# One instruction order for a whole gated attention and token-MLP kernel, with half-array projections, a GELU table and transposes by DMA

## The chip, the core and the metric

The kernel runs on one core of one Trainium2 chip, and the metric is the device time of one execution in microseconds. The core has TensorE (PE, the matrix array, which writes to eight banks of PSUM), VectorE (DVE), ScalarE (ACT) and GpSimd (POOL) for the rest of the arithmetic, and SyncE (SP), which here issues most DMA transfers. Each engine runs its own list of instructions in order and waits on semaphores for the others, so an instruction that waits holds back everything behind it on its engine.

## The reference

The input x has 2048 rows (tokens) of 448 features. A gate g mixes two branches, attention with a compressive memory (16 heads of 28 features, four segments of 512 tokens) and an MLP over the token axis after a layer norm:

```python
q, k, v = x @ wq, x @ wk, x @ wv          # split in 16 heads, 4 segments s
phi = lambda t: jnp.where(t > 0, t + 1.0, jnp.exp(t))
...
p = _softmax(qs @ ks.T * scale + causal_mask)
a_dot = p @ vs
a_mem = (phi(qs) @ M) / (phi(qs) @ z + 1e-06)
o = sigmoid(beta) * a_mem + (1.0 - sigmoid(beta)) * a_dot
M = M + phi(ks).T @ vs ; z = z + phi(ks).sum(rows)
...
a = o @ wo
u = _gelu(_layernorm(x).T @ w1 + b1)       # 448 x 1792, contracted over 2048 tokens
b = (u @ w2 + b2).T
g = _sigmoid((x * gate_w).sum(-1))
return g * a + (1 - g) * b
```

(This is the reference shortened; inputs and output are bf16.)

## The kernel before

The program calls `op(engine, function, reads, writes)` for every instruction group in program order; the small scheduler `Sched` derives the semaphores, and each engine's list is simply the order of those calls. So the order of the Python loops is the order on every engine.

There are two parts. **The front** (lines 508 to 536) runs over four blocks `tc` of 512 tokens. For each block `transposes` turns x with products against an identity (L359) and DVE copies the result out (L365); `do_k` and `do_q` (both through `proj_d`, L374) make K and Q with four chained products of 112 rows, transposed, a 512-token block by 128 columns, that is four heads padded from 28 to 32; `do_v` and `do_kt` (both through `proj_t`, L385) make V and a second, untransposed K. phi is computed as an exponential on ACT (L406, L427), a clamp on POOL (L408, L429) and a combine on DVE (L410, L431). `do_mst` (L444) adds phi(k)ᵀv to the memory. PSUM banks are taken in turn from all eight. After the last block `ln_coef` and sixteen `ln_apply` (L498 to L506) normalise x in place on POOL.

**The back half** is a loop of 50 slots. Each slot issues `scores` (L568), four products on four groups of array rows for four heads; then one `exp` over all four banks 0 to 3 on ACT (L577) and one or two causal masks on POOL (L582, L587). Every third slot `pv_unit` adds the product with V (L608, 16 products of 32 columns) and the division on DVE (L616 to L645), which writes the attention output over `qT`. Between them `mlp` issues an even share of 448 products: `mm1` (L656, u = w1ᵀx over 16 token tiles) and `mm2` (L689, y over 14 tiles of u). GELU is built by hand from ACT passes (Square L664, Identity L667, Tanh L675) and DVE passes (L670, L678). `wo_tile` (L720) and `final` (L728) join the branches, and SP stores 16 tiles (L731). The weights W1 and W2 come as 15 blocks of about 1 MB through a ring of five buffers (`ring_load`, L300 and L305).

In the profile most operands are called `t`, so groups are told apart by line.

## Time and profile before

| what | value |
|---|---|
| time, median of 3 runs (lowest to highest) | 258.96 us (258.67 to 259.0) |
| span of the profiled execution | 256.4 us |
| PE busy in the span | 201.7 us (79%) |
| DVE, ACT, POOL busy | 147.3 us, 140.5 us, 83.3 us |
| moved by DMA | 20.19 MB |

The span runs from the first to the last instruction of one profiled execution; the median of the runs is 2.6 us above it. Busy time of PE is not work at full speed: its clock has two levels, 1.2 and 2.4 GHz, which the profile shows as 0.50 and 1.00, and the records of products overlap, so the price of a group is read from the start of one group to the start of the next. Products of DVE, ACT and POOL show their own duration.

### The profile page before, as it was taken

How to read it: one execution, taken by the hardware profiler on the slowest of the kernel's cores; microseconds unless marked ns; L12 is line 12 of the kernel's file. 1: busy time of each engine (PE TensorE's matmuls, PEld its weight loads, DVE VectorE, ACT ScalarE, POOL GpSimd, SP SyncE). 2: the span in 40 equal slices, each digit the busy share in tenths (PEclk: the TensorE clock that was granted, in tenths of full speed). 3: DMA queues.
4: the chain of work that ended last, by engine and by line, in shares of the span. 5: the costliest groups of instructions: out<-in, count | busy, mean ns of one | idle time of the engine just before them, and what ended most of it. 6: DMA issues, size and time to landing. Idle time of an engine off the chain costs nothing.

```text
span 256.4 us, 3519 instructions
## 1 busy us (share of the span) xinstructions
PE 201.7 (79%) x1377; PEld 90.4 (35%) x1389; DVE 147.3 (57%) x265; ACT 140.5 (55%) x180; POOL 83.3 (32%) x122
## 2 busy tenths in 40 slices
PE   0499994996795028998989984995889898899893
PEld 0245551362352001233334431432343343334451
DVE  0426855944854700235567785974986677568703
ACT  0234614532641602389999986776766757756121
POOL 8001112301402099714443542340443223233000
PEclk9999998699799555589999998899999999999999
DMA  6999900000000000032632523145061460100102
GB/s 202 311 257 291 289 10 0 5 0 0 0 3 0 0 1 0 0 102 64 164 94 51 143 62 85 36 111 143 0 182 38 141 179 21 36 20 0 36 3 72
DMA packets 35908, 20.19 MB, mean 79 GB/s; under 512 B 1332, under 2 KB 35892, under 8 KB 35892
## 3 DMA queue, kind: packets, MB, share of 16 engines
q1 hardware_dynamic: 33328, 18.35, 26.5%
q10 hardware_dynamic: 2564, 1.62, 2.6%
q8 instruction: 11, 0.18, 0.3%
q14 instruction: 5, 0.04, 0.1%
HBM read 18.13 MB, written 1.84 MB: 78 GB/s over the span
## 4 chain that ended last, share of the span: by engine, by line
PE 39%; DVE 25%; ACT 18%; POOL 9%; issue 4%; DMA 3%; DVEq 0%; ACTq 0%
PE t L689 13%; ACT t L577 9%; PE t L374 6%; PE t L385 5%; PE t L656 5%; POOL t L506 4%; PE t L720 4%; DVE t L410 3%; DMA t<-in_A_wq_dram 3%; POOL t L408 3%; DVE t L402 3%; ACT t L406 3%; PE t L608 3%; PE t L568 2%; DVE t L728 2%
## 5 line engine op out<-in xcount | busy, mean ns | idle before, releaser
L577 ACT ACTIVATE t<-t 128x2048 bf16<-128x2048 f32 (+1 forms) x48 | 76.5, 1594 | 30.9 <-PE t L568 30.8
L656 PE MATMUL t<-t 128*128 128x448 bf16 x224 | 55.0, 382 | 10.4 <-POOL t L506 8.6
L689 PE MATMUL t<-t 128*128 128x448 bf16 x224 | 46.4, 353 | 0.0
L587 POOL TENSOR_SCALAR_AFFINE_SELECT t<-t 128x512 bf16<-128x512 bf16 x32 | 23.9, 748 | 50.4 <-ACT t L577 50.4
L582 POOL TENSOR_SCALAR_AFFINE_SELECT t<-t 128x512 bf16<-128x512 bf16 x32 | 24.2, 756 | 33.0 <-ACT t L577 31.9
L656 PEld LDWEIGHTS t<-t 128*128 128x128 bf16 x224 | 20.5, 101 | 38.0 <-issue 15.4
L374 PE MATMUL t<-t 112*128 112x512 bf16 x128 | 31.3, 401 | 3.3 <-DVE t L365 3.3
L385 PE MATMUL t<-t 112*128 112x449 bf16 (+1 forms) x112 | 26.7, 393 | 7.9 <-ACT t L406 6.5
L568 PE MATMUL t<-t 28*128 28x512 bf16 (+3 forms) x256 | 18.2, 319 | 16.1 <-ACT t L577 11.2
L689 PEld LDWEIGHTS t<-t 128*128 128x128 bf16 x224 | 20.2, 98 | 20.1 <-issue 2.6
L670 DVE SCALAR_TENSOR_TENSOR t<-t 128x448 f32<-128x448 f32 x14 | 9.2, 661 | 31.2 <-ACT t L667 31.1
L406 ACT ACTIVATE t<-t 128x512 bf16<-128x512 f32 x12 | 7.2, 597 | 27.6 <-DVE t L402 27.6
L728 DVE SCALAR_TENSOR_TENSOR t<-t 128x448 bf16<-128x448 f32 x16 | 10.5, 671 | 17.0 <-PE t L720 14.8
L408 POOL TENSOR_SCALAR t<-t 128x512 bf16<-128x512 bf16 x12 | 7.4, 613 | 38.6 <-ACT t L406 38.6
L374 PEld LDWEIGHTS t<-t 112*128 112x128 bf16 x128 | 12.9, 103 | 19.6 <-issue 3.6
L696 ACT ACTIVATE t<-t 128x448 bf16<-128x448 f32 x16 | 11.6, 722 | 14.7 <-PE t L689 14.7
L385 PEld LDWEIGHTS t<-t 112*128 112x128 bf16 x112 | 11.2, 105 | 21.4 <-DVE t L402 8.1
L410 DVE SCALAR_TENSOR_TENSOR t<-t 128x512 bf16<-128x512 bf16 x12 | 8.3, 692 | 17.9 <-POOL t L408 17.9
L568 PEld LDWEIGHTS t<-t 28*128 28x128 bf16 x256 | 5.2, 92 | 35.4 <-ACT t L577 21.8
L608 PE MATMUL t<-t 128*32 128x512 bf16 (+3 forms) x256 | 12.2, 312 | 6.8 <-DVE t L728 4.8
L429 POOL TENSOR_SCALAR t<-t 128x448 bf16<-128x448 bf16 x12 | 7.4, 616 | 25.9 <-ACT t L427 25.8
L402 DVE CAST t<-t 128x512 bf16<-128x512 f32 x16 | 11.0, 685 | 7.1 <-PE t L374 7.1
(70 smaller groups left out, 236.9 us busy)
## 6 DMA issues: line engine op xcount, KB each, us to landing
t<-in_B_w_dram SPq DMA_DIRECT2D x7, 1024.0 KB, 12.5
t<-in_B_w_dram SPq DMA_DIRECT2D x8, 896.0 KB, 5.1
t<-in_A_x_dram SPq DMA_DIRECT2D x4, 448.0 KB, 8.1
out_dram<-t SPq DMA_DIRECT2D x16, 112.0 KB, 1.7
t<-in_A_wk_dram ACTq DMA_DIRECT2D x1, 392.0 KB, 5.3
t<-in_A_wq_dram ACTq DMA_DIRECT2D x1, 392.0 KB, 7.9
...
```

What stands on the lines that cost most here:

```text
L374: last = e.matmul(bank(b)[:, 0:512], w_pad[0:CK, c, hg * 128 : hg * 128 + 128], xT[0:CK, c, tc * 512 : tc * 512 + 512], start=(c == 0), st ...
L385: last = e.matmul(bank(b)[:, 0:ncol], xT[0:CK, c, t * 128 : t * 128 + 128], w[0:CK, c, 0:ncol], start=(c == 0), stop=(c == NCT - 1), skip_ ...
L402: op("DVE", lambda e: e.tensor_copy(qs, bank(b)[:, 0:512]), reads=[R_bank[b]], writes=[R_qT[hg][tc]], name=f"cpq{tc}_{hg}")
L410: op("DVE", lambda e: e.scalar_tensor_tensor(phq[:, hg, (tc - 1) * 512 : tc * 512], qs, 0.0, eqt[:, p, :], op0=ALU.max, op1=ALU.add), read ...
L568: last = e.matmul(bank(hl)[:, c0 : c0 + w_], kT[r, hg, s * 512 + j * 128 : s * 512 + j * 128 + 128], qT[r, hg, s * 512 + 128 * j : s * 512 ...
L577: op("ACT", lambda e: e.activation(pv, ps[:, 0:4, 0:w], ACT.Exp, scale=SCALE), reads=R_bank[0:4], writes=[R_P[u % 2][f]] + alias, name=f"e ...
L582: op("POOL", lambda e, d=d: e.affine_select(d, d, pattern=[[0, 4], [1, 128]], compare_op=ALU.is_ge, fill=0.0, base=0, channel_multiplier=- ...
L587: op("POOL", lambda e: e.affine_select(d, d, pattern=[[0, 4], [1, 128]], compare_op=ALU.is_ge, fill=0.0, base=0, channel_multiplier=-1), r ...
L608: last = e.matmul(bank(CTX)[32 * hl : 32 * hl + 32, 128 * j : 512], vaug[:, 4 * s + j, 32 * h : 32 * h + 32], pv[:, hl, c0 : c0 + w_], sta ...
L656: op("PE", lambda e: e.matmul(bank(b)[:, 0:D], w1c[:, st, f2 * 128 : f2 * 128 + 128], xh[:, st, :], start=(st == 0), stop=(st == NT - 1), ...
L689: op("PE", lambda e: e.matmul(bank(b)[:, 0:D], w2c[:, ft, t2_ * 128 : t2_ * 128 + 128], uT[:, ft, :], start=(ft == 0), stop=(ft == NFT - 1 ...
L728: op("DVE", lambda e: e.scalar_tensor_tensor(outst[:, p, :], bank(b)[:, 0:D], gcol[:, T : T + 1], ybw[:, T % 4, :], op0=ALU.mult, op1=ALU. ...
```

## The change

The loops are gone. A text `PLAN` lists every step of the kernel once, as `name.arguments@engine`, and a loop at the end calls the function of each step in that order, so the plan alone sets the order on every engine, which engine takes a copy (ACT or DVE) and which PSUM bank or buffer a step uses. The steps themselves change as follows.

- K and Q are made together (`pair`): x is held transposed in both halves of the partitions, 7 chunks of 64 features each, in two different orders (`LC` and `UC`). The product of K runs on array rows 0 to 63 and that of Q on rows 64 to 127, alternating, into two banks. `v` does the same with two token tiles of V. The second projection of K is gone.
- phi is min(max(t,0)+1, exp(t)), on two head groups at a time (1024 columns): `pkm`/`pqm` on DVE or POOL, `pke`/`pqe` on ACT, `pkn`/`pqn` on DVE. phi(k) is turned by a DMA transpose in SBUF (`pkt`, 12 of them).
- x of block 0 is transposed on PE as before (`trx`, 28 products); blocks 1 to 3 are read from HBM with DMA transposes (`xtd`) and copied to the other half of the partitions by plain DMAs (`xtc`).
- Scores are packed into 40 fills of 4 x 512 columns (before 32 of 512 and 16 of 256), each with one `exp` and one mask.
- GELU is one table function over seven tiles of u at once (`gelu`, two calls); u leaves PSUM with its bias on DVE or ACT (`eu`).
- `ea` scales the attention part first and `fin` adds the MLP part; the last y tile is split in two halves of 224 columns.
- Eight products on zeros (`warm`) open the PE list; layer norm is done in four groups, its application shared between POOL and DVE; the ring has three buffers instead of five; PSUM banks 0 to 3 belong to the scores and 4 to 7 to all else.

```diff
+NWARM = 8
...
+LC = (5, 0, 2, 4, 6, 1, 3)
+UC = (6, 1, 3, 5, 0, 2, 4)
+GELU_BATCHES = ((0, 7), (7, 14))
...
+PLAN = """
+warm@P ldwk.0@A dve0@D id@G ldx.0@S ldx.1@S ldwq.0@A setup@G ldwk.1@S acttab@A ldwq.1@S ldsm@S xw.0@D bn.0@D trx.0.3@P
+trx.0.0@P trx.0.2@P trx.0.6@P bn.3@D trx.1.0@P trx.1.6@P trx.1.1@P trx.1.3@P ldwv.0@S trx.1.5@P ex.3@A trx.0.1@P
+xw.1@D trx.0.4@P pad.0@D trx.0.5@P ldwv.1@S trx.1.4@P trx.1.2@P ex.0@D ex.2@A xtd.1@S ex.1@D btr@P0 tb@A pad.1@D
...
+    def xtd(eng, u, tc):
+        b = tc % NXT
+        rows = slice(512 * tc, 512 * tc + 512)
+        dma(eng, xTb[:, b, 1:4, :], x2[rows, 0:384], writes=[R_xT[b][0], R_xT[b][2], R_xT[b][3]], group=f"xt{tc}",
+            transpose=True)
+        dma(eng, xTb[:, b, 0:1, :], x2[rows, 320:448], writes=[R_xT[b][0], R_xT[b][2], R_xT[b][3]], group=f"xt{tc}",
+            transpose=True)
...
+    def xtc(eng, u, tc):
+        b = tc % NXT
+        dma(eng, xTb[half[0], b, 4:7, :], xTb[half[1], b, 0:3, :], reads=[R_xT[b][0]], writes=[R_xT[b][1]],
+            group=f"xc{tc}")
+        dma(eng, xTb[half[1], b, 4:7, :], xTb[half[0], b, 1:4, :], reads=[R_xT[b][0]], writes=[R_xT[b][1]],
+            group=f"xc{tc}")
...
+    def warm(eng, u):
...
+            for _ in range(NWARM):
+                last = e.matmul(bank(7)[:, 0:512], dummy[:, 0:128], dummy[:, 128:640], start=True, stop=True,
                                 skip_group_check=True)
...
-    def proj_d(w_pad, R_w, hg, tc, b):
...
+            for t in (2 * h, 2 * h + 1):
...
-    def do_q(tc, hg):
-        b = next_bank()
-        p = hg % 2
-        proj_d(wq_pad, R_wqp, hg, tc, b)
-        qs = qT[:, hg, tc * 512 : tc * 512 + 512]
-        op("DVE", lambda e: e.tensor_copy(qs, bank(b)[:, 0:512]), reads=[R_bank[b]], writes=[R_qT[hg][tc]],
-           name=f"cpq{tc}_{hg}")
...
+    def pair(eng, u, tc, hg):
+        bk, bq = 4 + u[0], 4 + u[1]
+        slot["k", tc, hg], slot["q", tc, hg] = bk, bq
+        b = tc % NXT
+
+        def fn(e):
+            last = None
+            for i in range(7):
+                for h, c, bb in ((0, LC[i], bk), (1, UC[i], bq)):
+                    last = e.matmul(bank(bb)[:, 0:512], wkq[half[h], c, 128 * hg : 128 * hg + 128], xTb[half[h], b, i, :], start=(i == 0),
+                                    stop=(i == 6), skip_group_check=True)
+            return last
...
+    def v(eng, u, p):
+        t0 = 2 * p
+        bs = (4 + u[0], 4 + u[1])
+        slot["v", t0], slot["v", t0 + 1] = bs
+        b = (t0 // 4) % NXT
+
+        def fn(e):
+            last = None
+            for i in range(7):
+                for h in range(2):
+                    k0 = 128 * ((t0 + h) % 4)
+                    last = e.matmul(bank(bs[h])[:, 0 : D + 1], xTb[half[h], b, i, k0 : k0 + 128],
+                                    wvx[half[h], (LC, UC)[h][i], 0 : D + 1], start=(i == 0), stop=(i == 6),
...
-        op("ACT", lambda e: e.activation(eqt[:, p, :], bank(b)[:, 0:512], ACT.Exp), reads=[R_bank[b]],
-           writes=[R_eqt[p]], name=f"eq{tc}_{hg}")
-        op("POOL", lambda e: e.tensor_scalar(eqt[:, p, :], eqt[:, p, :], 1.0, 0.0, op0=ALU.min, op1=ALU.max),
...
+    def pmax(eng, dst, Rd, T, RT, hp, s):
+        op(eng, lambda e: e.tensor_scalar(dst.rearrange("p (g t) -> p g t", g=2), two(T, hp, s), 0.0, 1.0,
+                                          op0=ALU.max, op1=ALU.add),
+           reads=[RT[2 * hp][s], RT[2 * hp + 1][s]], writes=[Rd])
...
+    def pexp(i, T, RT, hp, s):
...
+    def pmin(dst, Rd, i):
+        op("DVE", lambda e: e.tensor_tensor(dst, dst, et[:, i, :], op=ALU.min), reads=[Rd, R_et[i]], writes=[Rd])
...
+    def pkt(eng, u, s, hg):
+        if hg == 0:
+            slot["kt", s] = u[0]
+        k, i = slot["kt", s], slot["kb", s, hg // 2]
+        dma(eng, phkT[:, k, :, hg * 128 : hg * 128 + 128], phk[:, i, 512 * (hg % 2) : 512 * (hg % 2) + 512],
+            reads=[R_phk[i]], writes=[R_phkT[k][hg]], transpose=True)
...
+    def fill(P, f):
+        a, b = 2 * (P % 2), 2 * (P % 2) + 1
+        return (((a, 0, 0, 512),), ((a, 3, 0, 128), (a, 1, 128, 384)), ((a, 2, 0, 256), (b, 2, 256, 256)),
...
+    def exp(eng, u, P, f):
+        i = slot["P", P, f] = u[0]
+        op("ACT", lambda e: e.activation(punit(i).rearrange("p (a q) -> p a q", a=4), ps[:, 0:4, :], ACT.Exp,
+                                         scale=SCALE),
+           reads=R_bank[0:4], writes=[R_P[i]] + (R_xT[i - NPX] if i >= NPX else []))
```

PE, the start of the program; L359 and `trx` (L518) are transposes, L374 and `pair` (L546) projections of K and Q, L385 and `v` (L571) those of V, L568 and `sc` (L695) scores. Before:

```order
L359 MATMUL t<-t 112x128 x16
L374 MATMUL t<-t 128x512 x32
L359 MATMUL t<-t 112x128 x16
L385 MATMUL t<-t 128x449 x4
L385 MATMUL t<-t 128x448 x4
```

After:

```order
L450 MATMUL t<-t 128x512 x8
L518 MATMUL t<-t 128x128 x28
L463 MATMUL t<-t 128x37
L546 MATMUL t<-t 128x512 x28
L571 MATMUL t<-t 128x449 x14
L546 MATMUL t<-t 128x512 x14
L695 MATMUL t<-t 128x512 x4
L571 MATMUL t<-t 128x449 x14
L546 MATMUL t<-t 128x512 x14
L695 MATMUL t<-t 128x128 x4
L695 MATMUL t<-t 128x384 x4
L546 MATMUL t<-t 128x512 x56
```

In the changed list scores stand between the projections of the first two blocks (from the seventh row on), and the 56 products of block 1 follow the second fill; before, scores begin only behind all four blocks.

SP's DMA queue, from the start (before) and behind the loads of the weights of V (after); `in_B_w_dram` are W1 and W2. Before:

```order
L271 DMA t<-in_A_x_dram 128x4x448 x4
L300 DMA t<-in_B_w_dram 128x16x256 x7
L305 DMA t<-in_B_w_dram 128x14x256 x5
L731 DMA out_dram<-t 128x448
L305 DMA t<-in_B_w_dram 128x14x256
```

After:

```order
L357 DMA_TRANSPOSE t<-in_A_x_dram 128x3x512
L357 DMA_TRANSPOSE t<-in_A_x_dram 128x1x512
L357 DMA t<-in_A_x_dram 128x4x448
L357 DMA t<-t 64x1536 x2
L357 DMA t<-in_B_w_dram 128x16x256
L357 DMA t<-in_A_x_dram 128x4x448
L357 DMA_TRANSPOSE t<-in_A_x_dram 128x3x512
L357 DMA_TRANSPOSE t<-in_A_x_dram 128x1x512
L357 DMA t<-in_A_x_dram 128x4x448
L357 DMA_TRANSPOSE t<-t 128x4x128
L357 DMA t<-t 64x1536 x2
L357 DMA t<-in_B_w_dram 128x16x256
```

The ring's first block (the fifth row) now stands behind a transposed read of x and the two copies that wait for it, and the second block behind a transposed phi(k).

ACT, in the middle of the MLP; L577 and L705 are the exponentials, L664, L667 and L675 the GELU passes, L848 `gelu`, L839 `eu`. Before:

```order
L577 ACTIVATE t<-t 128x1024
L664 ACTIVATE t<-t 128x448
L667 ACTIVATE t<-t 128x448
L577 ACTIVATE t<-t 128x2048
L675 ACTIVATE t<-t 128x448
L577 ACTIVATE t<-t 128x2048
L664 ACTIVATE t<-t 128x448
```

After:

```order
L705 ACTIVATE t<-t 128x2048
L591 ACTIVATE t<-t 128x1 x2
L705 ACTIVATE t<-t 128x2048 x2
L848 ACT_TABLE_LOAD
L848 ACTIVATE t<-t 128x3136
L839 ACTIVATE t<-t 128x448
L705 ACT_TABLE_LOAD
L705 ACTIVATE t<-t 128x2048 x2
```

Three passes for each u tile between the exponentials are replaced by one pass over 3136 columns, with a table load on each side of it.

## Rows read from the trace of the kernel before

**Rows 1.** The page: busy time by engine; PE's busy tenths and clock by slice.
```profile
PE 201.7 (79%) x1377; PEld 90.4 (35%) x1389; DVE 147.3 (57%) x265; ACT 140.5 (55%) x180; POOL 83.3 (32%) x122
...
PE   0499994996795028998989984995889898899893
...
PEclk9999998699799555589999998899999999999999
```

**Rows 2.** Windows: length, busy us of PE, PEld, DVE, ACT, POOL; clock; DMA share; GB/s.
```profile
0.00:95.00 95.00, 64.75 (x358) 31.90 (x358) 49.89 (x109) 34.59 (x75) 25.60 (x44) 0.88 0.37 92
95.00:106.00 11.00, 9.16 (x29) 1.94 (x29) 0.00 (x0) 2.34 (x2) 11.00 (x17) 0.50 0.00 0
106.00:186.00 80.00, 67.63 (x535) 28.53 (x539) 53.75 (x85) 66.96 (x73) 29.89 (x40) 0.95 0.31 85
186.00:252.00 66.00, 59.93 (x459) 28.02 (x464) 41.43 (x68) 36.33 (x32) 16.79 (x24) 1.00 0.22 64
```

**Rows 3.** The chain that ended last, in order of time: start, us, what.
```profile
1.27 7.91 DMA t<-in_A_wq_dram
...
11.08 9.04 PE t L374 x32
...
69.81 3.46 PE t L374 x16
73.27 0.91 PE t L444 x16
...
93.70 11.20 POOL t L506 x16
```

**Rows 4.** Waits: who waited for whom; us in total, times, longest.
```profile
POOL t L408 <- ACT t L406: 38.6, 12, 6.8
```

**Rows 5.** Timeline of PE in the steady part: start, us, line, shapes, count.
```profile
195.65 0.73 PE L608 MATMUL t<-t 128*32 128x512 bf16 x16 [0.25 <-POOL t L587]
196.31 1.69 PE L689 MATMUL t<-t 128*128 128x448 bf16 x8
197.84 0.92 PE L720 MATMUL t<-t 128*128 128x448 bf16 x4
198.69 0.29 PE L568 MATMUL t<-t 28*128 28x256 bf16 x4
198.91 1.69 PE L689 MATMUL t<-t 128*128 128x448 bf16 x8
200.53 0.39 PE L568 MATMUL t<-t 28*128 28x512 bf16 x4
200.86 1.69 PE L689 MATMUL t<-t 128*128 128x448 bf16 x8
```

**Rows 6.** Groups by line and shape: busy us, mean ns of one, then idle before.
```profile
L577 ACT ACTIVATE t<-t 128x2048 bf16<-128x2048 f32 x32 | 60.1, 1878 | 21.1 <-PE t L568 21.0
...
L582 POOL TENSOR_SCALAR_AFFINE_SELECT t<-t 128x512 bf16<-128x512 bf16 x32 | 24.2, 756 | 33.0 <-ACT t L577 31.9
...
L577 ACT ACTIVATE t<-t 128x1024 bf16<-128x1024 f32 x16 | 16.4, 1025 | 9.9 <-PE t L568 9.8
...
L667 ACT ACTIVATE t<-t 128x448 f32<-128x448 f32 x14 | 8.8, 630 | 0.0
...
L498 POOL TENSOR_TENSOR t<-t 128x16 f32<-128x16 f32 x1 | 2.9, 2942 | 0.1
...
L394 ACT ACT_TABLE_LOAD x1 | 1.3, 1283 | 7.8 <-issue 7.8
```

**Rows 7.** DMA issues: count, KB each, us to landing.
```profile
t<-in_A_x_dram SPq DMA_DIRECT2D x4, 448.0 KB, 8.1
...
t<-in_gate_w_dram ACTq DMA_DIRECT2D x1, 0.9 KB, 10.8
```

**Rows 8.** Timeline of the end: start, us, engine, line, count.
```profile
251.75 2.46 DVE L728 SCALAR_TENSOR_TENSOR t<-t 128x448 bf16<-128x448 f32 x4 [7.79 <-PE t L720]
252.46 2.11 SPq L731 DMA_DIRECT2D out_dram<-t  x4
```

More of the change, by code (lines that the diff above doesn't have):

```diff
@@ new lines, in ldwo @@
+    def ldwo(eng, u):
+        for hl in range(4):
+            dma(eng, wo_sb[32 * hl : 32 * hl + DH, :, :], WO.rearrange("(g l d) m -> l d g m", g=NHG, l=4)[hl],
+                reads=[R_woz], writes=[R_wo], group="wo")
+    def xtd(eng, u, tc):
[5 more added lines that the diff above has]
+            transpose=True)
@@ L382, in fn, with xw, trx @@
+    R_xw = R("xw", 4)
+    def xw(eng, u, h):
+        r = slice(2 * h, 2 * h + 2)
+        op("DVE", lambda e: e.tensor_copy(x0[:, r, D:512], x0[:, r, 0:64]), reads=R_x[r], writes=R_xw[r])
+    def trx(eng, u, h, i):
+        b, c0 = i // 2, (i % 2) * 512
         def fn(e):
             last = None
-            for c in range(NCT):
-                last = e.matmul(bank(b)[:, 0:ncol], xT[0:CK, c, t * 128 : t * 128 + 128], w[0:CK, c, 0:ncol],
-                                start=(c == 0), stop=(c == NCT - 1), skip_group_check=True)
@@ L753, in build_kernel @@
[L753 to L758 removed]
+            for hg in range(NHG):
+                last = e.matmul(bank(b)[:, 0:D], oT[:, hg, T * 128 : T * 128 + 128], wo_sb[:, hg, :], start=(hg == 0),
+                                stop=(hg == NHG - 1), skip_group_check=True)
+            return last
+        op("PE", fn, reads=[R_qT[hg][T // 4] for hg in range(NHG)] + [R_wo], writes=[R_bank[b]])
@@ L760, in build_kernel @@
+    engines = dict(P="PE", A="ACT", D="DVE", G="POOL", S="SP")
+    op("DVE", lambda e: e.memset(dummy[:], 0.0), writes=[R_dummy])
+    for item in PLAN.split():
+        what, where = item.split("@")
+        name, *args = what.split(".")
+        emit_op[name](engines[where[0]], [int(c) for c in where[1:]], *[int(a) for a in args])
     totals = sch.finalize()
```

888 lines of the change are left out of this document (455 added, 433 removed).

## The prediction

> **What bounds the kernel now.** I read the page first. PE is busy for 201.7 of 256.4 us, more than any other engine, but its slices fall to 0, 2 and 4 tenths between 80 and 100 us, and its clock row falls to 5 in several places before slice 19 [rows 1]. So I cut the span by windows [rows 2]. From 0 to 95 us PE is busy for 64.75 us, with no engine above that: the front is a chain, not a load. From 95 to 106 us POOL is busy for all 11.00 us at a granted clock of 0.50. From 106 to 252 us PE is busy for 67.63 + 59.93 = 127.6 of 146 us, with ACT next in the first part (66.96 of 80).
>
> The chain in order of time says what the front waits for [rows 3]: the weights of Q until 9.18 us, 32 projections from 11.08 us that take 9.04 us (0.28 us each, where 16 later ones take 3.46 us, 0.216 us each), and at 93.70 us sixteen layer-norm passes on POOL for 11.20 us. In between, the phi steps go round three engines: POOL's clamp waited 38.6 us for ACT's exponential, in 12 pieces [rows 4]. Nothing of the MLP, 448 products, runs in that time. The changed order puts the front's work, the scores and the MLP side by side. If that works, the bound is the sum of PE's own work.
>
> **What PE's work costs at the full clock.** I price from start to start in the timeline [rows 5]. Eight MLP products take 196.31 to 197.84, 1.53 us, so 0.191 us each. Four output products take until 198.69, 0.85 us. Sixteen products with V take 0.66 us. A score fill of four products of 512 columns takes 0.33 us, although four in a row at 0.216 us would take 0.86 us: products on different row groups do run side by side here, and a group costs 0.12 us above one product. Before a score fill the eight MLP products take 198.91 to 200.53, 1.62 us, so entering another split of the array costs 0.09 us more. With these:
>
> - u and y: 448 x 0.191 = 85.6 us, unchanged.
> - `pair`: 16 groups of 7 double products. Side by side: 7 x 0.216 + 0.12 + 0.09 = 1.72 us, 27.5 us in all. One behind the other: 14 x 0.216 + 0.21 = 3.23 us, 51.7 us. The trace shows no 64-row product; the nearest row is the score fill of 28-row products [rows 5], which ran side by side, so I take 27.5 us.
> - `v`: 8 groups, 7 x 0.191 + 0.21 = 1.55 us, 12.4 us (or 23.1 us one behind the other).
> - Scores: 40 fills x (0.33 + 0.09) = 16.8 us. Products with V: 16 x (0.66 + 0.09) = 12.0 us.
> - wo: 16 x 0.85 = 13.6 us. Memory update: 3 x 0.91 [rows 3] = 2.7 us. Memory reads: 12 x 0.216 = 2.6 us.
>
> Sum: 173.2 us. For the old order the same prices give the work behind 106 us as 132 us (85.6 for the MLP, 18.4 for 32 fills of 512 and 16 of 256 columns, 12.0, 13.6 and 2.6) in 146 us, so that part had about 14 us of waits, 10%.
>
> **Ahead and behind.** Q's weights landed at 9.18 us and the first projection ran at 11.08 us [rows 3]. Now the first half of the columns of K and Q is loaded first, and the pads and the 28 transposes follow; I take 10.5 us to the first `pair` (9 to 14). The first projections before ran at 0.28 us instead of 0.216 us for 32 products [rows 3], 2 us lost to the low clock. With `warm` and the transposes ahead I take half, 1 us (0 to 2.5). Behind the last product, the old kernel has four final passes (251.75 to 254.21) and four stores (252.46 to 254.57), and ends at 256.4 [rows 8], so one store takes 256.4 - 254.57 = 1.8 us from the end of its issue. Only two half tiles remain now: about 0.8 + 0.5 + 1.8 = 3.1 us.
>
> **The other engines must fit below PE's 173 us.** ACT: exponentials cost 60.1 + 16.4 us; 40 of 1.878 us are 75.1 us [rows 6]. The GELU passes go, 42 of about 0.61 us (one kind is 0.630 us [rows 6]), 26 us. In their place come two table passes. From 1024 to 2048 columns the exponential rises from 1.025 to 1.878 us, 0.833 ns a column, so 3136 columns cost 2.8 us; with four table loads of 1.283 us that is 10.7 us. With fewer evictions ACT falls from 140.5 us [rows 1] to some 120 us. DVE loses 28 GELU and 24 phi passes and gains about as many (evictions, `eu`, `ea`, the phi maxima and minima), so it stays near its 147.3 us [rows 1], 80% of the time that remains. POOL keeps its masks (0.756 us for 512 columns [rows 6], the same number of columns), loses 24 clamps and half of the layer-norm passes, and gains phi maxima and three more groups of coefficients. The power there took 2.942 us for 16 columns [rows 6]; for 4 columns I take 1.5 us (0.3 to 2.9). It stays near 83 us. So none of the three passes PE in the whole, but DVE comes close, and in order.
>
> The table loads have cover: both exponentials around `gelu` and `eu` (0.63 us) make 1.9 + 1.28 + 2.8 + 0.6 + 1.28 + 1.9 = 9.8 us on ACT, and PE has 44 MLP products, two groups with V, a memory update and a fill in that stretch, 8.4 + 1.5 + 0.9 + 0.4 = 11.2 us. The row shows 1.283 us for a load [rows 6]. The Trainium skill ("ScalarE: Activation LUTs", What ACT_TABLE_LOAD costs) gives about 2.66 us for a switch, with a drain in it. By it the stretch would take 12.5 us, and the two stretches together would cost about 3 us of stall; no trace here shows the drain.
>
> **The DMA transposes.** They are new, and SP issues them in order, with the ring's blocks, the copies and the later loads of x behind them. Block 1 of x must have been turned and copied before its first `pair`. PE has the four `pair` and two `v` of block 0 and two fills to do by then, 6.9 + 3.1 + 0.8 = 10.8 us, so until about 21 us. The nearest rows are plain loads of x, 448 KB landing 8.1 us after issue with others ahead [rows 7], and, at the far end, the gate weights, 0.9 KB in two-byte pieces landing after 10.8 us in the same queue time. A turned block is 512 KB. With issue at about 8 us, 8 us to land and 2 to 3 us for the copies, it is there at 19 us, just in time. I take 0 us, with 0 to 14 us for the range. The Trainium skill ("DMA: Bandwidth & Descriptors", Latency and other measured facts) gives 261 GB/s for a transposing DMA; by it a block would take 2 us of transfer, an estimate, and the sum would stay as it is.
>
> **Waits.** The old back part lost 10%, much of it to ACT, which was busy 66.96 of 80 us [rows 2] and is relieved. But DVE is as full as before and each engine takes its list in order. I take half the old share, 5% of 173 us, 8.7 us (2% to 12%, 3.5 to 21 us).
>
> **Sum.** 10.5 + 1 + 173.2 + 8.7 + 3.1 = 196.5 us of span. The profiled span of before is 2.6 us below the median of the runs, so the forecast is **199 us**.
>
> **Rivals.**
> 1. *The halves don't run side by side* (the change doesn't do what it says). For: no 64-row product is in the trace, and two of them load two sets of weights for each column pass. Against: the score fill and the sixteen products with V [rows 5]. Price: 24.2 + 10.7 = 35 us of PE, 234 us.
> 2. *The first 40 us starve PE*: x turned late, POOL's coefficients (four powers of up to 2.9 us) ahead of the first layer norms, DVE with its statistics between evictions. PE's work up to the sixth score fill is 10 `pair`, 3 `v`, 5 fills, 26 MLP products and one group with V, 17.2 + 4.7 + 2.1 + 5.0 + 0.8 = 29.8 us; at the old front's density (64.75 of 95 us [rows 2]) it takes 43.7 us, so 14 us more: 213 us.
> 3. *Slower: the transposes hold SP's queue.* If they go in small pieces like the gate weights [rows 7], x of blocks 1 to 3, 1.5 MB, comes late, and the ring's blocks stand behind. The last turned block is needed some 45 us into the span, so the three have cover for some 40 us. Slower than before needs 60 us more, so 1.5 MB in over 100 us, below about 15 KB a us, where the plain load of x made 448 KB in 8.1 us, 55 KB a us. At 10 KB a us it is 150 us, 110 us uncovered, and 309 us.
>
> **How the numbers follow.** Forecast (190 to 206 us) 0.62; starved start or more waits on DVE (206 to 222 us) 0.18; below 190 us, if the group overheads of 0.21 us on some 80 groups are half hidden and waits are 2%, 0.07; halves in turn 0.09; slower 0.03; the same 0.01. The range goes from 186 us (199 less 5 of waits and 8 of overhead) to 222 us (199 with 14 us at the start and 9 us more of waits); it leaves out the halves in turn, the slower case and a little below. Faster by over 0.2%, about what a measurement of this kernel can tell from no change: 0.96; within it 0.01; slower 0.03.
>
> **What the profile after would show.** Seven double projections start to start in about 1.7 us, not 3.2; PE busy in every slice from the fifth on, with the clock at 1.00 from about 15 us; scores from about 18 us on; ACT near 120 us and DVE near 147 us; the first `pair` of block 1 waiting for little or nothing on `xtd` or `xtc`; about 9 us of waits spread over many places. I am wrong if DVE or ACT is 95% busy over tens of us with PE waiting, or if PE waits for a DMA in the first 50 us by more than a few us.

## The result, and the profile after

| what | before | after |
|---|---|---|
| time, median (lowest to highest) | 258.98 us (258.67 to 259.42) | 201.6 us (199.02 to 202.29) |
| ratio to before, 95% interval | 1 | 0.7717 (0.7672 to 0.7761) |
| span of the profiled execution | 256.4 us | 197.3 us |
| mean granted clock of PE in it | 0.920 | 0.983 |
| PE, DVE, ACT, POOL busy | 201.7, 147.3, 140.5, 83.3 us | 176.7, 143.8, 118.5, 84.4 us |

The time falls by 57.4 us, from 258.98 to 201.6 us, where the forecast was 199 (186 to 222). The two longest of the four runs, 202.25 and 202.29 us, are those with the lowest mean clock, 0.957, and the ratio leaves them out; differences between kernels below are taken between the medians of the runs that count for the ratios, here 199.02 and 200.95 us, 200.0 in the median. The profiled execution is the 199.02 us one, so 1.7 us lie outside its span.

The page after, as [rows 1]: busy time by engine, PE's busy tenths and clock in 40 slices (4.9 us each), and the shares of the chain that ended last by line.

```profile
PE 176.7 (90%) x1464; PEld 79.9 (40%) x1471; DVE 143.8 (73%) x272; ACT 118.5 (60%) x108; POOL 84.4 (43%) x85
...
PE   7399993999599989989399997999999999999994
...
PEclk9999999699999999999969999999999999999999
...
PE t L884 14%; POOL t L609 13%; PE t L831 10%; PE t L857 4%; POOL t L718 4%; PE t L736 3%; DVE t L367 3%; DVE t L618 3%; DVE t L791 3%; DMA t<-in_A_beta_dram 2%; PE t L695 2%; PE t L571 2%; POOL t L819 2%; DVE t L870 2%; SPq L357 2%
```

The valley between 80 and 106 us in [rows 1] and [rows 2] is gone. Counted from 0, PE's weak slices ahead of the last are now the first two, 6, 10 and 19, and the clock falls to 6 tenths in 7 and 20, right behind two of them. In the chain stands one line that the prediction gave no price: the maximum of phi on POOL (L609), 13% of the span.

PE's timeline (start, us, line, shapes, count, and in brackets the idle time ahead with its releaser). L546 is `pair`, L571 `v`, L695 `sc`, L831 `u`, L749 `mem`, the read of the memory:

```profile
9.76 0.19 PE L463 MATMUL t<-t 37*128 37x37 bf16 x1 [1.91 <-DMA t<-in_A_beta_dram]
9.85 1.69 PE L546 MATMUL t<-t 64*128 64x512 bf16 x14
11.82 1.69 PE L546 MATMUL t<-t 64*128 64x512 bf16 x14 [0.28 <-DVE t L469]
...
16.30 0.40 PE L695 MATMUL t<-t 28*128 28x512 bf16 x4
...
20.50 6.25 PE L546 MATMUL t<-t 64*128 64x512 bf16 x56 [0.26 <-ACT t L587]
26.58 1.50 PE L571 MATMUL t<-t 64*128 64x449 bf16 x14
...
34.91 1.27 PE L831 MATMUL t<-t 128*128 128x448 bf16 x4 [3.83 <-POOL t L819]
...
36.65 2.71 PE L546 MATMUL t<-t 64*128 64x512 bf16 x14
...
42.53 1.69 PE L546 MATMUL t<-t 64*128 64x512 bf16 x14
44.15 0.39 PE L695 MATMUL t<-t 28*128 28x512 bf16 x4
...
53.49 1.50 PE L571 MATMUL t<-t 64*128 64x449 bf16 x14 [2.10 <-DVE t L367]
54.92 0.93 PE L831 MATMUL t<-t 128*128 128x448 bf16 x4
...
98.71 0.39 PE L749 MATMUL t<-t 128*128 128x512 bf16 x1 [3.23 <-DVE t L842]
```

Fourteen products of 64 rows take 42.53 to 44.15, 1.62 us, and four such steps in a row take 20.50 to 26.58, 1.52 us each. One behind the other, 14 products would take 14 x 0.216 = 3.02 us [rows 3], so the halves do run side by side. The three long waits are 3.83, 2.10 and 3.23 us. Behind the first of them the step at 36.65 takes 2.65 us to the next one (39.30): there the clock is low (slice 7), and behind the third it is low again (slice 20).

Groups of the profile after, as [rows 6] (busy us, mean ns of one, then idle before): masks, the maximum of phi on POOL, the GELU table, the power of the layer norm.

```profile
L718 POOL TENSOR_SCALAR_AFFINE_SELECT t<-t 128x1024 bf16<-128x1024 bf16 (+1 forms) x40 | 38.0, 951 | 65.4 <-ACT t L705 61.0
L609 POOL TENSOR_SCALAR t<-t 128x1024 bf16<-128x1024 bf16 x7 | 26.5, 3795 | 1.6 <-DVE t L367 1.1
...
L848 ACT ACTIVATE t<-t 128x3136 bf16<-128x3136 bf16 x2 | 5.6, 2818 | 0.0
L811 POOL TENSOR_TENSOR t<-t 128x4 f32<-128x4 f32 x4 | 4.4, 1108 | 0.3
```

And the same instruction on two engines, from the view of one line: lowest, median and highest ns, first and last start.

```profile
L609 POOL TENSOR_SCALAR t<-t x7: 3619/3729/4059, 28.0 to 118.5; 128x1024 bf16<-128x1024 bf16 x7
L609 DVE TENSOR_SCALAR t<-t x5: 417/427/1253, 15.3 to 81.4; 128x1024 bf16<-128x1024 bf16 x5
```

A maximum and an addition over 1024 columns take 3.7 us on POOL and 0.43 us on DVE in the median. What that does to the layer norms of block 1 is seen in POOL's timeline ahead of PE's wait at 34.91:

```profile
28.00 4.06 POOL L609 TENSOR_SCALAR t<-t 128x1024 bf16<-128x1024 bf16 x1
...
32.42 1.03 POOL L811 TENSOR_TENSOR t<-t 128x4 f32<-128x4 f32 x1
...
34.13 1.42 POOL L819 TENSOR_SCALAR t<-t 128x448 bf16<-128x448 bf16 x2
```

`pqm.1.1` stands in POOL's list ahead of the coefficients (`lnc`, L811) and layer norms (`lna`, L819) of the next block of x, and PE's `u` products wait for the first of those. How much of the 3.83 us the maximum makes, the first experiment shows.

### The profile page after: what moved, and what is told of

The parts are those of the page before. It is cut to its first block, busy times and chain, and to the rows that moved or that the text cites. A ratio compares the mean times of both kernels' runs of the same rounds, so it can differ in the third digit from the quotient of the medians.

```text
span 197.3 us, 3599 instructions
## 1 busy us (share of the span) xinstructions
PE 176.7 (90%) x1464; PEld 79.9 (40%) x1471; DVE 143.8 (73%) x272; ACT 118.5 (60%) x108; POOL 84.4 (43%) x85
## 4 chain that ended last, share of the span: by engine, by line
PE 38%; DVE 25%; POOL 23%; issue 6%; DMA 2%; SPq 2%; ACT 2%; another core or an unknown queue 0%; POOLq 0%; DVEq 0%
PE t L884 14%; POOL t L609 13%; PE t L831 10%; PE t L857 4%; POOL t L718 4%; PE t L736 3%; DVE t L367 3%; DVE t L618 3%; DVE t L791 3%; DMA t<-in_A_beta_dram 2%; PE t L695 2%; PE t L571 2%; POOL t L819 2%; DVE t L870 2%; SPq L357 2%
## 5 line engine op out<-in xcount | busy, mean ns | idle before, releaser
L705 ACT ACTIVATE t<-t 128x2048 bf16<-128x2048 f32 x40 | 75.1, 1877 | 30.8 <-PE t L695 28.2
L718 POOL TENSOR_SCALAR_AFFINE_SELECT t<-t 128x1024 bf16<-128x1024 bf16 (+1 forms) x40 | 38.0, 951 | 65.4 <-ACT t L705 61.0
L831 PE MATMUL t<-t 128*128 128x448 bf16 x224 | 49.8, 361 | 3.9 <-POOL t L819 3.8
L884 PE MATMUL t<-t 128*128 128x448 bf16 (+1 forms) x238 | 45.9, 342 | 0.1
L831 PEld LDWEIGHTS t<-t 128*128 128x128 bf16 x224 | 19.9, 99 | 27.5 <-issue 7.4
L884 PEld LDWEIGHTS t<-t 128*128 128x128 bf16 x238 | 22.6, 98 | 20.2 <-issue 2.3
L546 PE MATMUL t<-t 64*128 64x512 bf16 x224 | 27.5, 388 | 0.7 <-DVE t L469 0.3
L609 POOL TENSOR_SCALAR t<-t 128x1024 bf16<-128x1024 bf16 x7 | 26.5, 3795 | 1.6 <-DVE t L367 1.1
L365 ACT ACTIVATE t<-t 128x512 bf16<-128x512 f32 (+3 forms) x27 | 15.7, 599 | 12.8 <-PE t L546 6.0
L367 DVE CAST t<-t 128x512 bf16<-128x512 f32 (+1 forms) x23 | 15.0, 654 | 8.0 <-PE t L546 6.1
L618 DVE TENSOR_TENSOR t<-t 128x1024 bf16<-128x1024 bf16 x12 | 13.7, 1158 | 4.2 <-POOL t L609 4.1
L546 PEld LDWEIGHTS t<-t 64*128 64x128 bf16 x224 | 10.4, 96 | 15.5 <-issue 3.1
L695 PE MATMUL t<-t 28*128 28x512 bf16 (+3 forms) x256 | 16.1, 304 | 0.1
L571 PE MATMUL t<-t 64*128 64x449 bf16 x112 | 12.0, 350 | 2.8 <-DVE t L367 2.1
L857 PE MATMUL t<-t 128*128 128x448 bf16 x64 | 13.8, 354 | 0.0
L842 DVE TENSOR_SCALAR t<-t 128x448 bf16<-128x448 f32 x10 | 6.7, 673 | 8.9 <-PE t L831 8.9
L614 ACT ACTIVATE t<-t 128x1024 bf16<-128x1024 bf16 x12 | 12.3, 1060 | 0.0
```

Source lines behind the costliest of these rows:

```text
L367: op(eng, lambda e: e.tensor_copy(out, in_), reads=reads, writes=writes)
L546: last = e.matmul(bank(bb)[:, 0:512], wkq[half[h], c, 128 * hg : 128 * hg + 128], xTb[half[h], b, i, :], start=(i == 0), stop=(i == 6), sk ...
L571: last = e.matmul(bank(bs[h])[:, 0 : D + 1], xTb[half[h], b, i, k0 : k0 + 128], wvx[half[h], (LC, UC)[h][i], 0 : D + 1], start=(i == 0), s ...
L609: op(eng, lambda e: e.tensor_scalar(dst.rearrange("p (g t) -> p g t", g=2), two(T, hp, s), 0.0, 1.0, op0=ALU.max, op1=ALU.add), reads=[RT[ ...
L618: op("DVE", lambda e: e.tensor_tensor(dst, dst, et[:, i, :], op=ALU.min), reads=[Rd, R_et[i]], writes=[Rd])
L695: last = e.matmul(bank(hl)[:, c0 : c0 + w], kT[r, hg, s * 512 + j * 128 : s * 512 + j * 128 + 128], qT[r, hg, s * 512 + 128 * j : s * 512 ...
```

## The experiments

After the result my theory had three parts. (1) Most of the gain is the order: MLP work stands where the front used to wait. (2) The shorter steps, K and Q side by side and no second K, are a smaller part. (3) What stays above the ideal is some 13 us of waits of PE, mostly behind the slow maximum on POOL. The rivals were that the halves do the main part, that the clock or the DMA transposes set the time, and that the POOL passes are covered.

### The maximum of phi, moved from POOL to DVE

```diff
- ... pqm.1.1@G1 ... pkm.1.0@G1 ... pkm.1.1@G0 ... pqm.2.0@G2 ... pkm.2.1@G0 ... pqm.3.0@G0 ... pqm.3.1@G1
+ ... pqm.1.1@D1 ... pkm.1.0@D1 ... pkm.1.1@D0 ... pqm.2.0@D2 ... pkm.2.1@D0 ... pqm.3.0@D0 ... pqm.3.1@D1
```

> All seven phi maxima that ran on POOL (3.8 us each, 26.5 us in all) run on DVE, where the same step took 0.43 us in the median; nothing else moves. Theory (the three long PE waits of 3.83, 2.10 and 3.23 us all go back to a phi maximum on POOL that stands ahead of a layer-norm pass, a mask or a division): these 9.2 us of waits fall below 3 us, and the low-clock stretches behind two of them go as well, so the time falls by 8 to 12 us, to about 190 to 193 us. Rival (DVE, 73% busy, is the real limit and the waits only move): DVE gets 3 us more work in places where it is already late, PE still waits 7 us or more in all after 30 us, and the time falls by less than 4 us.

Measured: 193.26 us (191.6 to 194.98), ratio 0.7492 (0.7449 to 0.7535), 6.9 us below the changed kernel where I expected 8 to 12. POOL falls to 58.2 us of busy time and DVE to 141.1. The wait of 3.83 us becomes 1.77, and that of 2.10 us is gone, but the third is still there. PE's timeline of this kernel:

```profile
34.02 1.07 PE L831 MATMUL t<-t 128*128 128x448 bf16 x4 [1.77 <-POOL t L819]
...
94.08 0.39 PE L749 MATMUL t<-t 128*128 128x512 bf16 x1 [3.17 <-DVE t L842]
```

So seven instructions cost about 7 us of the time, and the third wait is another matter: a read of the memory waits until an eviction of `u` (`eu.8`, L842) frees its PSUM bank, and `eu.8` stands on DVE behind the joins and transposes of the attention output. The two waits give 2.06 + 2.10 us, so part (3) of my theory held for a third of the 13.2 us of waits. Another part is the clock, the last column but two in these windows. The changed kernel, in the columns of [rows 2]:

```profile
34.50:39.50 5.00, 4.59 (x24) 1.40 (x24) 3.37 (x5) 1.88 (x1) 4.65 (x8) 0.66 0.65 134
98.70:103.60 4.90, 4.89 (x32) 1.68 (x33) 2.10 (x4) 3.33 (x3) 0.63 (x1) 0.65 0.11 28
```

And this one:

```profile
30.00:40.00 10.00, 7.53 (x66) 2.92 (x63) 9.55 (x23) 5.88 (x5) 7.65 (x13) 1.00 1.06 197
94.00:106.00 12.00, 11.92 (x106) 6.05 (x107) 9.60 (x19) 9.69 (x6) 3.10 (x4) 1.00 0.33 89
```

In the 10 us of the changed kernel about 3.4 us are lost, 10 x 0.34, an estimate. With the two waits that is 7.6 us, and the two profiled spans lie 7.4 us apart (197.3 and 189.9 us).

### Why POOL is slow there: the order of the two operations, or the shape

Two runs change one thing each in `pmax`. The first turns the operations round, max(t + 1, 1), which gives the same values; the second makes, on POOL only, two flat instructions of 512 columns in place of one over 2 x 512.

```diff
-        ... two(T, hp, s), 0.0, 1.0, op0=ALU.max, op1=ALU.add
+        ... two(T, hp, s), 1.0, 1.0, op0=ALU.add, op1=ALU.max
```

> The phi maximum is computed as max(t + 1, 1) instead of max(t, 0) + 1, on the same engines and shapes. If the order of the two operations is what makes POOL slow (3.8 us for 1024 columns, where a clamp of 512 columns took 0.61 us in the kernel before), the POOL instances fall to about 1.2 us and the time to about 191 to 194 us. If it is not the operations but the shape or the width, they stay at 3.6 to 4.1 us and the time stays at 199 to 203 us.

Measured: 198.24 us (197.61 to 198.86), ratio 0.7662 (0.7619 to 0.7705), which overlaps that of the changed kernel, with the instruction at 3726 ns in the median: no change.

```diff
+        for g in range(2 if eng == "POOL" else 1):
+            if eng == "POOL":
+                d, sr = dst[:, 512 * g : 512 * g + 512], T[:, 2 * hp + g, s * 512 : s * 512 + 512]
```

> In the changed kernel each phi maximum on POOL is issued as two instructions of 512 columns in a row, instead of one over two stretches of 512 columns that lie 2048 apart; the operations are the same. If the view with two stretches is what costs POOL 3.7 us, an instruction takes about 0.6 to 0.7 us, as the clamp of the kernel before did for the same width, and the time falls to about 191 to 195 us. If it is the pair of operations (a maximum and an addition, in either order), an instruction takes about 1.8 us and the time stays near 199 to 202 us.

Measured: 205.83 us in a single run, above the 199 to 202 that I expected; its three long waits are 4.24, 2.96 and 3.53 us, and one run doesn't settle more. For the instruction, in the same view as above:

```profile
L614 POOL TENSOR_SCALAR t<-t x14: 1917/1918/2355, 29.3 to 127.0; 128x512 bf16<-128x512 bf16 x14
```

Half the columns take half the time, so neither the shape nor the order of the operations is the cause. The clamp of the kernel before, a minimum and a maximum over 512 columns of the same type on the same engine, took 0.613 us in the mean of its twelve. It differs in two ways: in its pair of operations, and in that it writes over its own input, where `pmax` writes to another tile. Which of the two makes `pmax` three times as slow on POOL no run here separates.

### The halves one behind the other

```diff
-            for i in range(7):
-                for h, c, bb in ((0, LC[i], bk), (1, UC[i], bq)):
+            for h in range(2):
+                for i in range(7):
+                    c, bb = (LC, UC)[h][i], (bk, bq)[h]
```

(and the same in `v`.)

> In each projection step the seven products of the lower half of the array rows are issued first and then the seven of the upper half, instead of in alternation; same products, same banks. Theory (the two halves run side by side only because neighbours in the list lie on different halves): a K and Q step grows from 1.6 to about 3.1 us and a V step from 1.4 to about 2.8 us, so PE gets 16 x 1.5 + 8 x 1.35 = 35 us more work and the time rises by 28 to 38 us, to about 230 to 240 us. Rival (the hardware overlaps them in any order, or the two halves share something and gain little from alternation): the steps stay under 2.2 us and the time rises by less than 10 us.

Measured: 209.85 us (206.87 to 211.3), ratio 0.805 (0.7979 to 0.8122), 8.3 us more than the changed kernel. I expected 28 to 38 us more, so my theory that the two halves overlap only between neighbours in the list fell. PE's timeline of this kernel (L547 `pair`, L572 `v`, L696 `sc`):

```profile
14.71 0.35 PE L572 MATMUL t<-t 64*128 64x449 bf16 x1
14.73 0.38 PE L547 MATMUL t<-t 64*128 64x512 bf16 x1
14.90 0.35 PE L572 MATMUL t<-t 64*128 64x449 bf16 x1
...
23.26 7.00 PE L547 MATMUL t<-t 64*128 64x512 bf16 x56
29.92 0.36 PE L572 MATMUL t<-t 64*128 64x449 bf16 x1
...
49.28 2.35 PE L547 MATMUL t<-t 64*128 64x512 bf16 x14
51.56 0.39 PE L696 MATMUL t<-t 28*128 28x512 bf16 x4
```

At 14.71 us the last products of a `pair`, all on the upper half, run between the first products of the `v` behind it, on the lower half. A step by itself takes 2.28 us (49.28 to 51.56) where 14 in strict turn would take 3.02, and four in a row take 1.665 us each (23.26 to 29.92). So a product on a free half starts beside those of the other half that stand ahead of it in the list. Writing them alternately is worth 0.66 us for a step by itself and 0.15 us within a row.

### Both chains on one half

To see what the step costs if the halves really don't overlap, both chains go to the lower half.

```diff
-                for h, c, bb in ((0, LC[i], bk), (1, UC[i], bq)):
+                for h, c, bb in ((0, LC[i], bk), (0, LC[i], bq)):
```

> Both chains of every projection step run on the lower half of the array rows, in the same alternation and into the same two banks. V stays what it was; Q is made from K's weights, so the attention is another one, with the same shapes and counts. Theory (the two chains run side by side because they lie on different row groups, whatever their order in the list, which is why issuing the halves in turn cost only 8 us): without different row groups a K and Q step takes 14 x 0.216 = 3.0 us or more instead of 1.6, a V step 2.7 us instead of 1.4, PE gets 16 x 1.4 + 8 x 1.3 = 33 us more work, and the time rises by 25 to 38 us, to about 227 to 240 us. Rival (the steps are not bound by the array but by loading weights or by PSUM): the steps stay near 1.6 us and the time near 201 us.

Measured: 256.16 us (256.08 to 256.24), ratio 0.9894 (0.9876 to 0.9913), 56.2 us more than the changed kernel, where I expected 25 to 38. The page of this kernel, PE's busy tenths and its clock, and the step in its timeline:

```profile
PE   7699999999999999999999969999899899999995
...
PEclk9855555555558999999999997999999999999999
```

```profile
38.35 6.18 PE L546 MATMUL t<-t 64*128 64x512 bf16 x14
44.46 0.61 PE L695 MATMUL t<-t 28*128 28x128 bf16 x8
```

The step takes 6.11 us, 14 products of 0.436 us, twice 0.218: one behind the other, at a clock of 0.50. At the full clock it would be 3.05 us, so the prediction's price of the rival (3.23 us a `pair`) was about right: 16 x (3.05 - 1.62) = 23 us, and 8 x (14 x 0.191 - 1.43) = 10 us for `v`. The rest goes with the clock: in slices 2 to 11 (12.7 to 76 us) it stays at the low level although PE is busy in every slice. By estimate, these 63.6 us at 0.50 lose 31.8 us, where the changed kernel lost 3.4; against that, PE's waits behind the first `pair` fall from 13.2 to 4.9 us. So 33 + 31.8 - 3.4 - 8.3 = 53 of the 57 us between the two profiled spans are accounted for. I hadn't expected the low clock, nor do these runs say why it lasts.

### The same steps, the front first

This kernel has all steps of the changed kernel, in the same forms, but the plan lists the projections, phi, the memory and the layer norms ahead of all scores and MLP products, as the loops of the kernel before did. Within each of the two parts the order is that of the changed plan; the diff shows one row of it.

```diff
- sc.0.0@P gt.1@A eq.0.3@A v.0@P12 ek.0.3@D exp.0.0@A0 bn.7@D pair.0.2@P30 ldx.3@S bn.5@D ev.0@D ev.1@A mask.0.0@G
+ gt.1@A eq.0.3@A v.0@P12 ek.0.3@D bn.7@D pair.0.2@P30 ldx.3@S bn.5@D ev.0@D ev.1@A
...
```

> The same steps on the same engines, but all projection, phi, memory and layer-norm steps of the four blocks stand first in the plan and the scores, MLP and output steps follow, each group in its own order; one buffer of phi(q) is then overwritten too early, so the memory part of some units is another one, at the same cost. Theory (the order is what keeps PE fed, since the front needs some 60 us of DVE for 41 us of PE): the front ends at 65 to 80 us instead of being spread over 115 us, PE waits 15 to 25 us in it, and the time rises by 8 to 20 us, to 210 to 222 us. Rival (the shorter steps alone explain the gain): the time stays below 206 us.

Measured: 252.79 us (248.43 to 254.25). The shortest run, which is the profiled one, is 48 us above the changed kernel and 10.5 us below the kernel before. PE's timeline of it:

```profile
33.83 2.79 PE L548 MATMUL t<-t 64*128 64x512 bf16 x14 [4.63 <-ACT t L589]
41.49 3.15 PE L548 MATMUL t<-t 64*128 64x512 bf16 x14 [4.88 <-DVE t L369]
...
84.64 0.40 PE L697 MATMUL t<-t 28*128 28x512 bf16 x4
```

And the first score fill of the kernel before:

```profile
85.31 0.61 PE L568 MATMUL t<-t 28*128 28x512 bf16 x4 [4.62 <-ACT t L406]
```

The front waits for its PSUM banks to be emptied, 29 us in all, and the steps behind the longest waits run at the low clock (2.8 and 3.2 us in place of 1.69, with a mean clock of 0.59 and 0.50). The scores begin at 84.64 us, and the second fill waits 3.22 us for an exponential. So the shorter steps alone didn't shorten the front: the scores of the kernel before begin at 85.31 us. In this order the shorter steps are worth about 10 us, and about 48 of the 59 us (258.98 to 200.0) are the order. The split holds for this one order only. It keeps the changed plan's engines and its four banks for the front, where the kernel before takes all eight in turn, so a better front-first order might lose less; and no run has the old steps in the new order. I had expected 8 to 20 us, far too little: each wait of the front is short, but nothing else stands behind it in PE's list, and the clock falls behind it.

### GELU by table in the kernel before

```diff
-        op("ACT", lambda e: e.activation(gg[:, q, :], bank(b)[:, 0:D], ACT.Square, bias=b1s[:, ft : ft + 1],
...
+        op("DVE", lambda e: e.tensor_scalar_add(uT[:, ft, :], bank(b)[:, 0:D], b1c[:, ft : ft + 1]), ...
+        if ft % 7 < 6:
+            return
...
+            op("ACT", lambda e: e.activation(t, t, ACT.Gelu_apprx_tanh), ...
```

> The kernel before with one part of the change alone: u leaves PSUM with its bias on DVE, and the table GELU runs over seven tiles at a time, instead of three ACT and two DVE passes for each tile. Theory (the parts are worth little in the old order, where the front is a chain without the MLP and PE's work behind it is unchanged): ACT loses 20 us of work, but the time falls by 2 to 8 us only, to 251 to 257 us. Rival (ACT was the limit of the first part of the MLP): the time falls by 12 us or more.

Measured: 262.22 us (260.87 to 262.62), ratio 1.0122 (1.009 to 1.0153): 3.2 us slower, where I had expected a gain of 2 to 8. ACT's busy time does fall, from 140.5 to 130.6 us, and DVE's from 147.3 to 138.4. Timelines of ACT and of PE in this kernel:

```profile
136.25 1.28 ACT L671 ACT_TABLE_LOAD   x1
137.55 2.82 ACT L671 ACTIVATE t<-t 128x3136 bf16<-128x3136 bf16 x1
140.38 1.28 ACT L577 ACT_TABLE_LOAD   x1
```

```profile
143.61 0.61 PE L568 MATMUL t<-t 28*128 28x384 bf16 x8 [4.88 <-ACT t L577]
...
145.88 3.17 PE L656 MATMUL t<-t 128*128 128x448 bf16 x8
```

Two loads and one pass make 5.4 us in which ACT does no exponential. In the loop of slots the next score fill stands behind the slot's eight MLP products, so PE waits 4.88 us for the banks, and the clock is low behind that: eight MLP products take 3.1 us at 145.88 in place of 1.53 [rows 5]. The second table pass costs 1.27 us of wait at 179.56 and leads to 2.07 more. But the score fills of the kernel before waited for exponentials too, and longer in sum. The waits (us in total, times, longest) before:

```profile
PE t L568 <- ACT t L577: 11.2, 12, 3.1
```

And in this kernel:

```profile
PE t L568 <- ACT t L577: 9.1, 10, 4.9
```

So there are fewer of these waits but a longer one, and what grows is PE's busy time, from 201.7 to 208.3 us for the same products. The mean clock, 0.913 where it was 0.920, makes some 2 us of that, an estimate (8.7% of 259.9 us against 8.0% of 256.4); what makes the rest is open. The changed plan has the same two passes with the same durations (2818 ns) and PE waits for neither; around the first it puts 44 MLP products and two groups with V. That agrees with the cover that the prediction named, but the two kernels differ in more than this, and no run takes the cover alone away. The Trainium skill's 2.66 us for a switch ("ScalarE: Activation LUTs", What ACT_TABLE_LOAD costs), with a drain of 1.38 us in it, isn't seen: the pass starts 0.02 us behind the 1.28 us load and the next load 0.01 us behind the pass.

### The first steps and the transposes

```diff
- warm@P ldwk.0@A dve0@D ...
+ ldwk.0@A dve0@D ...
```

> The eight products on zeros at the start of PE's list are left out; they compute nothing that is used. Theory (they are why the first projections at 9.85 us ran at the full rate, 1.6 us a step, while the first 16 to 20 products before ran at half rate): the first steps then take up to 3.1 us until the clock has risen, and the time rises by 1.5 to 5 us. Rival (the transposes and the projections bring the clock up by themselves): the first step takes 1.6 us and the time changes by less than 1 us.

Measured: 200.63 us (198.81 to 203.79), ratio 0.7688 (0.7655 to 0.7722), which overlaps that of the changed kernel. Without the eight `warm` products the first two `pair` take 4.6 us (9.93 to 14.53) and not 3.5, and block 1 starts at 21.73 in place of 20.50; the end doesn't move. Nor is `warm` a sure cure: with it, the first two `pair` of the kernel with DVE's maxima took 4.7 us (10.11 to 14.81). So it is worth 1.2 us there at best, and other work takes that up. (In the kernel before, 32 products in 9.04 us [rows 3] leave room for about 10 at half rate, not the 16 to 20 of the expectation.)

```diff
-        dma(eng, xTb[:, b, 1:4, :], x2[rows, 0:384], ..., transpose=True)
+        dma(eng, xTb[:, b, 1:4, :].rearrange(...), x4[:, :, 0:384], ...)
```

(and the same for the second part of `xtd` and for `pkt`: 18 transposes become plain copies of as many bytes.)

> All 18 DMA transposes are plain copies of the same number of bytes between the same buffers, so K, Q, V of blocks 1 to 3 and the memory are made from untransposed data; everything else is as in the changed kernel. Theory (the transposes take SP 5 to 7 us a block to issue and the DMA engines much of the first 60 us, but no PE wait names them): the DMA share of the first 40 us falls, the first projection of block 1 starts within 1 us of 20.5 us, and the time stays within 2.5 us of 201.6 us. Rival (they hold back the ring's blocks or the layer-norm loads, and the long waits go back to them): the waits at 31 to 35 us shrink and the time falls by 4 us or more.

Measured: 202.49 us (202.26 to 202.71), ratio 0.7821 (0.7807 to 0.7836), 2.5 us more than the changed kernel. The three long waits of PE are those of the changed kernel (3.83, 2.42 and 3.23 us). The first 40 us of the changed kernel and of this one, in the columns of [rows 2]:

```profile
0.00:40.00 40.00, 31.23 (x253) 13.00 (x257) 34.48 (x86) 21.56 (x29) 20.86 (x37) 0.96 1.02 210
```

```profile
0.00:40.00 40.00, 32.72 (x243) 14.75 (x245) 33.83 (x85) 21.56 (x29) 20.01 (x36) 0.89 0.97 233
```

The DMA engines are full in both (shares of 1.02 and 0.97), and block 1's first `pair` starts at 20.50 and 21.33. The mean clock of these 40 us is 0.89 in place of 0.96, which goes with the 2.5 us; why it is lower isn't shown. So turning the data costs nothing above a plain copy of as many bytes. What the bytes themselves cost no run here tells.

### A better version

Four moves in the plan: the maxima on DVE (as above); `eu.8` ahead of `ot.4` on DVE; the statistics `bn.8` ahead of `pkn.0.1` on DVE; the transposition of beta and the biases (`btr`) behind the first `pair` on PE.

```diff
- ... ot.4@D u.4.8@P ... exp.3.4@A3 eu.8@D mem.6@P30
+ ... eu.8@D u.4.7@P ot.4@D u.4.8@P ... exp.3.4@A3 mem.6@P30
- ... v.3@P21 pkn.0.1@D ... pqm.1.1@G1 bn.8@D
+ ... v.3@P21 bn.8@D pkn.0.1@D ... pqm.1.1@D1
- btr@P0 tb@A pad.1@D pair.0.1@P12 gcp@D
+ tb@A pad.1@D pair.0.1@P12 btr@P0 gcp@D
```

> Phi maxima on DVE as before (193.3 us in the median), and three moves in the plan: the eviction of u tile 8 stands before the turns of units 4 and 5 on DVE, so that its PSUM bank is free sooner; the statistics of x tile 8 stand before a phi minimum, so that POOL's third group of layer-norm coefficients starts sooner; the transposed biases follow the first projection instead of standing ahead of it. Theory (each of the remaining PE waits of 3.17, 1.77 and 2.10 us is held by the step named): the waits fall to below 1.2 us each and the time falls by 3 to 7 us, to 186 to 190 us. Rival (another step of the same engine is late next, or the low clock takes the gain): the time falls by less than 2 us.

Measured: 191.17 us (190.82 to 191.44), ratio 0.7385 (0.7374 to 0.7395), 1.9 us below the kernel with DVE's maxima alone. PE's timeline:

```profile
12.91 1.69 PE L546 MATMUL t<-t 64*128 64x512 bf16 x14 [1.90 <-DVE t L469]
...
32.41 1.07 PE L831 MATMUL t<-t 128*128 128x448 bf16 x4 [0.43 <-POOL t L819]
...
92.39 0.39 PE L749 MATMUL t<-t 128*128 128x512 bf16 x1 [0.67 <-DVE t L842]
```

The third wait falls from 3.17 to 0.67 us, which shows that `eu.8`'s place in DVE's list was its cause. The first falls from 1.77 to 0.43 us: what was left of it without the maximum was the place of the statistics `bn.8` on DVE. The move of `btr` brings the first `pair` from 10.11 to 9.31 us, but the second one now waits 1.90 us for the copies behind `btr` on DVE (L469), and at 46.35 us a `pair` waits 1.47 us for the minimum of phi. I expected 3 to 7 us and got 1.9.

A last kernel also puts the second part of the bias copies (`b2c`) directly behind the first:

```diff
- gcp@D b1c@D bn.2@D ldx.2@S bn.1@D b2c@D eq.0.1@A
+ gcp@D b1c@D b2c@D bn.2@D ldx.2@S bn.1@D eq.0.1@A
```

> The four moves plus one: the copy of the second bias out of PSUM stands directly behind that of the first, ahead of the statistics of x tiles 1 and 2 on DVE, so that the bank of the transposed biases is free for the second projection. Theory (that bank is what the second projection waits 1.90 us for): that wait falls below 0.8 us and the time falls by 0.8 to 2 us, from 191.2 to about 189.5 us. Rival (the evictions behind it on DVE are late next): the time falls by less than 0.5 us.

Measured: 190.37 us (189.52 to 191.93), ratio 0.7365 (0.7336 to 0.7393). The interval overlaps that of the kernel before it, so its 0.8 us isn't settled; the wait at the second `pair` fell to 0.43 us. It is the fastest of these kernels, 68.5 us below the kernel before and 9.6 us below the changed one.

## Why the prediction was right, step by step

| term | predicted | after |
|---|---|---|
| start of the first `pair` | 10.5 (9 to 14) | 9.85 |
| low clock at the start | 1 (0 to 2.5) | 0 here, 0 to 1.2 in other runs |
| PE's work | 173.2 | 171.7 |
| waits | 8.7 (3.5 to 21) | 13.2 |
| behind the last product | 3.1 | 2.6 |
| span | 196.5 | 197.3 |
| outside the span | 2.6 | 1.7 |

The work is what is left: the last product ends at 194.74 us, and 194.74 - 9.85 - 13.16 = 171.7. The waits are the sum of the ten that the timeline shows behind the first `pair`. That the span came out within 0.8 us is in part luck: the waits were 4.5 us too small, and start, low clock, work and end together 3.7 us too large.

- **The bound.** Right. The front was a chain, and its time went once other work stood beside it: PE's waits fell to 13 us, and with the front first again 48 us came back. PE is busy for 90% of the span.
- **Halves side by side.** Right, and the price was near: 1.62 us for a `pair` by itself, 1.52 in a row, 1.72 predicted; 1.43 for `v`, 1.55 predicted. The 0.09 us for entering another split of the array was too much. Together that is some 3 us less work, and the two stretches at the low clock (slices 7 and 20) took it back: two times 5 us at 0.65 are 3.4 us lost. The sum of the work is right partly because these two cancel.
- **Waits.** The term that was mis-sized, 13.2 us where I took 8.7. Half of the old back part's share was a guess about the whole, while the largest single cause was an operation that I left without a price: POOL "gains phi maxima", I wrote, and set them against the clamps that go, as if they cost alike. They take 3.8 us each, 26.5 us in all, and made 2.06 + 2.10 = 4.2 us of the waits. The next were two places in DVE's list: `eu.8` (3.23 us, 0.67 once moved) and the statistics `bn.8` (1.77 us, 0.43 once moved). POOL's total came out right (84.4 where I said near 83) because the masks fell from 48.1 to 38.0 us on wider tiles and the old clamps and layer norms went: a right total with a wrong make-up. That POOL is 43% busy told nothing of what stood behind those seven instructions in its list.
- **Signs.** PE was to be busy in every slice from the fifth on, with the clock at 1.00 from about 15 us and the waits spread over many places. Slices 6, 10 and 19 stand at 3, 5 and 3 tenths, the clock fell twice, and three waits make 9.2 of the 13.2 us.
- **The other engines.** ACT 118.5 us (some 120 predicted), DVE 143.8 (near 147). The table pass was priced at 2.8 us and took 2.818; the power of 4 columns took 1.108 us (1.5, 0.3 to 2.9).
- **DMA.** Right: the transposes cost no more than plain copies of as many bytes, and the first `pair` of block 1 waited 0.26 us, on ACT's copy and not on a transpose. A turned part of x, of which a block has two, lands 5.1 us after issue in the median; I took 8 for a block.
- **Start.** Better by 0.65 us; what ended it was not the weights but the 4 KB of beta, for which PE waited 1.91 us ahead of the first `pair`. The 2 us that I put down to the low clock in the kernel before aren't seen in its clock, which the profile gives as 1.00 from 11 to 20.2 us; what it shows is the slower products.
- **Rivals.** The halves in turn: refuted by the 1.62 us step; the kernel on one half shows that the price in the prediction was right at the full clock and too small in fact, since the clock stayed low. The starved start: the 3.83 us at 35 us are of this kind, where it asked for 14, half through POOL's list, by a maximum and not by the powers (1.1 us each), and half through DVE's statistics, which the rival named. The slow transposes: refuted.
- **Two readings of [rows 1].** Between 77 and 103 us PE's slices stand at 5, 0, 2 and 8 tenths (the 4 is slice 6, near 40 us), and the clock's 5 is one stretch, slices 13 to 16. Neither enters the sum.
